# Reordering the first batch of an attention and MLP kernel: pooled k ahead of v, weight transposes during the divisions, and earlier scores in the later batches

## Chip, cores and metric

The kernel runs on one core of one Trainium2 chip. The metric is device time in microseconds (us), median over several executions; lower is better. Marks and durations come from one profiled execution of each kernel, which is about 1.8 us shorter than its time (374.2 against 375.95 us for the kernel before).

## The reference

For each of 8 batches, attention with keys and values mean-pooled over 8 neighbouring rows, then a residual MLP block that mixes first tokens, then channels:

```python
# q, k, v: (8, 8, 576, 64)
k_p = k.reshape(B, H, 72, 8, D).mean(axis=3)
v_p = v.reshape(B, H, 72, 8, D).mean(axis=3)
scores = np.matmul(q, k_p.transpose(0, 1, 3, 2)) / np.sqrt(D)
attn = softmax(scores)                       # (8, 8, 576, 72)
x = np.matmul(attn, v_p).transpose(0, 2, 1, 3).reshape(8, 576, 512)

tok = np.einsum('ts,bsd->btd', w_tok, alpha1 * x + beta1)
u   = x + lam * tok
ch  = np.maximum((alpha2 * u + beta2) @ w_ch1, 0) @ w_ch2   # 512 -> 2048 -> 512
out = u + lam * ch
```

## The kernel before

The order of instructions is written by hand. Batch 0 is a straight list, the opening. Then nine blocks of 512 tokens pass through the MLP (`mlp_A` is the first layer, `mlp_B` the second), and the attention of the next batch is woven between a block's matmuls at fractional slot numbers: slots 0 to 15 are the first layer, 16 to 31 the second.

| line | engine | work |
|---|---|---|
| L115, L117, L118 | GpSimd | `cast_rem`: the last 64 rows ("remainder") of q cast, of k summed |
| L132, L133 | VectorE or GpSimd | `sum_k`: rows of k summed in groups of 8 |
| L391, L395 | TensorE, copies | `att_K`: pooled k of four heads into its layout |
| L403, L405; L411, L415 | sums; TensorE, copies | `sum_v`, `att_V`: the same for v |
| L421, L422; L429, L431 | GpSimd; TensorE, copies | `sum_v_rem`, `att_Vrem`: remainder of v |
| L440, L442 | TensorE, ScalarE | `att_S`: scores and exponentials of a head |
| L457/L460, L462, L464 | TensorE, VectorE | `att_AV`: product with v, reciprocal, division into `x_tm` |
| L471, L475 | VectorE or GpSimd | `att_X`: `xs`, two heads of x times a row vector |
| L261 | VectorE | `row_of_xs`: one row of xs, from vectors alone |
| L276, L279 | TensorE, ScalarE | `setup_wtok`: token-mix weights transposed |
| L505, L520 | TensorE | `mix_T`, `mix_uT`: the token mix, and its result transposed |
| L536, L541; L559 | TensorE, ScalarE; TensorE | first layer and its relu; second layer |

The parts that the change touches:

```python
    def load_rem(b):
        raw = work.tile([P, 2, 4, D], FP, tag="rem_raw", bufs=2, name="rem_raw")
        for i, src in enumerate((q, k)):
            nc.sync.dma_start(out=raw[:, i]..., in_=src[b, :, 512:576, :]...)   # 128 KB each
# ...
    load_qk(0, 0)          # q and k of heads 0-3, 512 KB each
    load_rem(0)
    load_qk(0, 1)
    load_v(0, 0)
    load_v_rem(0)
    load_v(0, 1)
# ... the opening, from the first scores on
    sum_k(0, 1, nc.vector)
    att_F(0, 1)                            # q of heads 4-7 transposed
    att_S(0, 2)
    att_S(0, 3)
    sum_v(0, 0)
    att_Vrem(0, nc.scalar.copy)
    att_K(0, 1, nc.scalar.copy)
    att_V(0, 0, nc.vector.tensor_copy)
    sum_v(0, 1, nc.gpsimd)
    att_S(0, 4)
    att_AV(0, 0)
# ... heads 4 to 7 and the other products
    att_X(0, 4, 6, nc.gpsimd)
    load_w2(0)                             # 512 KB, a quarter of w_ch2
    setup_wtok(0, nc.scalar.copy)
    att_AV(0, 6)
    load_qk(1, 0, nc.vector)               # and the other loads of batch 1
# ...
    setup_rowsum(0)
    setup_wtok(2, nc.scalar.copy)
    setup_rowsum(1)
    setup_wtok(3, nc.scalar.copy)
    mix_T(0, 0)
    setup_rowsum(2)
    mix_T(0, 1)
    setup_rowsum(3)
    setup_vectors()
    mix_T(0, 2, nc.gpsimd)
# ... the later batches
    def attention(b):
        late = b == 1
        todo = [(2.0 if late else -2.0, lambda: cast_rem(b, nc.gpsimd)),
# ...
        for h in range(8):
            at = 13.6 + 1.0 * h if late else 13.1 + 1.0 * h
            todo.append((at, lambda h=h: att_S(b, h)))
            todo.append((at + 2.0, lambda h=h: att_AV(b, h)))
            if h % 2:
                todo.append((at + 2.1, lambda h=h: att_X(b, h - 1, h + 1)))
```

The softmax here doesn't subtract the row's maximum and nothing guards it: scores larger than these inputs give would overflow.

## Time and profile before

| | kernel before |
|---|---|
| time, median of 3 | 375.79 us (375.37 to 376.31) |
| span of the profiled execution | 374.2 us |
| busy: TensorE, VectorE, ScalarE, GpSimd | 355.8, 226.9, 203.8, 98.8 us |

I read this profile by marks: moments at which a stage starts on TensorE, found in its timeline. There are seven: first reciprocal (first L462), mix (first L505), A (first matmul of the first layer), B (first of the second layer), F2 and F7 (first transposes, L357, of q of batches 2 and 7), and the end. The sum of busy time is of less use. It comes from matmul records, and the trace of before lacks 43 of 2344.

### The profile page before, as it was taken

Reading aid. Unit: us, or ns where it says so; the run is one execution under the profiler, and the core shown is the slowest. Engines: PE = TensorE matmul, PEld = TensorE weight load, DVE = VectorE, ACT = ScalarE, POOL = GpSimd, SP = SyncE. Lnnn points to the kernel's source line nnn. Section 1 sums busy time; section 2 is a strip of 40 time slices with the busy share of each in tenths; the row PEclk is TensorE's granted clock in tenths of the full one; section 3 lists DMA queues with packets and bytes.
Section 4 is the critical chain, followed back from the end, with each engine's and each line's share of the span. In section 5 each row is a group of like instructions: output and inputs, shape, how many; then the busy total and the mean of one; then the engine's idle time right before and its main releaser. Section 6 shows DMA issues by size and latency. Waiting matters only on the chain.

```text
span 374.2 us, 6081 instructions
## 1 busy us (share of the span) xinstructions
PE 355.8 (95%) x2301; PEld 197.2 (53%) x2344; DVE 226.9 (61%) x468; ACT 203.8 (54%) x408; POOL 98.8 (26%) x145
## 2 busy tenths in 40 slices
PE   6589899999999999999999999999999999999995
PEld 2357555455545554555545554555455545544544
DVE  6585349783797269744985299428853797633011
ACT  4765885069704981399227941796159704712710
POOL 7774939004600470019000910073000000000000
PEclk9989999999999999999999999999999999999999
DMA  7999991039011912084016502480100011002002
GB/s 240 249 213 318 309 309 53 2 118 341 33 58 59 335 45 58 28 275 133 30 56 227 182 29 58 132 276 30 56 28 3 1 58 56 2 28 84 2 30 83
DMA packets 19602, 43.27 MB, mean 116 GB/s; under 512 B 2221, under 2 KB 4593, under 8 KB 19574
## 3 DMA queue, kind: packets, MB, share of 16 engines
q1 hardware_dynamic: 17488, 37.89, 29.9%
q0 software_dynamic: 1920, 4.86, 6.9%
q8 instruction: 18, 0.29, 0.3%
q10 hardware_dynamic: 166, 0.14, 0.1%
q14 instruction: 10, 0.08, 0.1%
HBM read 38.30 MB, written 9.44 MB: 128 GB/s over the span
## 4 chain that ended last, share of the span: by engine, by line
PE 77%; DVE 12%; DMA 5%; SPq 2%; ACT 1%; issue 1%; POOL 1%; POOLq 0%
PE ps_h L536 32%; PE ps_ch L559 25%; PE ps_tok L505 11%; DVE x_tm L464 5%; DVE xs L471 3%; PE ps_sc L440 3%; DMA rem_raw<-in_k_dram 2%; DMA rem_v_raw<-in_v_dram 2%; PE ps_uT L520 2%; PE ps_q L357 2%; DVE rec L462 1%; DVE xs L475 1%; PE ps_av L457 1%; SPq L78 1%; PE ps_kp L388 1%
## 5 line engine op out<-in xcount | busy, mean ns | idle before, releaser
L536 PE MATMUL ps_h<-u_fm,w 128*128 128x512 bf16 (+1 forms) x574 | 133.2, 373 | 1.0 <-ACT u_fm L522 0.2
L559 PE MATMUL ps_ch<-w,Hj 128*128 128x512 bf16 x493 | 123.2, 379 | 0.9
L541 ACT ACTIVATE Hj<-ps_h,bias_cols 128x512 bf16<-128x512 f32 x144 | 96.7, 691 | 38.2 <-PE ps_h L536 23.2
L536 PEld LDWEIGHTS <-w 128*128 128x128 bf16 x592 | 64.9, 114 | 48.0 <-issue 0.4
L559 PEld LDWEIGHTS <-Hj 128*128 128x128 bf16 x592 | 55.6, 98 | 48.6 <-issue 0.5
L522 ACT COPY u_fm<-ps_uT 128x512 bf16<-128x512 bf16 x36 | 21.1, 586 | 91.1 <-PE ps_uT L520 91.1
L442 ACT ACTIVATE ET<-ps_sc 128x288 f16<-128x288 f32 (+1 forms) x128 | 52.7, 488 | 12.5 <-PE ps_sc L440 11.8
L505 PE MATMUL ps_tok<-xs,wtT 128*128 128x512 bf16 (+1 forms) x196 | 48.5, 379 | 2.6 <-DVE xs L471 2.3
L395 DVE CAST kpT<-ps_kp 64x288 bf16<-64x288 f32 x29 | 13.2, 455 | 54.3 <-PE ps_kp L391 54.1
L115 POOL CAST rem_q<-rem_raw 128x256 bf16<-128x256 f32 x8 | 3.2, 398 | 140.3 <-DMA rem_raw<-in_q_dram 84.9
L566 DVE TENSOR_TENSOR u_sb<-u_sb,ps_ch 128x512 f32<-128x512 f32 (+1 forms) x37 | 24.9, 672 | 24.9 <-PE ps_ch L559 23.8
L565 DVE TENSOR_TENSOR ps_ch<-lam_bc,ps_ch 128x512 f32<-128x512 f32 x32 | 22.1, 691 | 19.8 <-PE ps_ch L559 19.5
L507 DVE TENSOR_TENSOR u_sb<-x_tm,ps_tok 128x512 f32<-128x512 f32 (+1 forms) x40 | 27.3, 684 | 10.4 <-PE ps_tok L505 10.3
L464 DVE TENSOR_TENSOR x_tm<-ps_av,rec 128x320 f32<-128x320 f32 x64 | 31.4, 491 | 2.3
L505 PEld LDWEIGHTS <-wtT 128*128 128x128 bf16 (+1 forms) x200 | 19.1, 98 | 25.2 <-issue 2.8
L440 PE MATMUL ps_sc<-qT,kpT 128*128 128x288 bf16 (+1 forms) x128 | 28.5, 306 | 2.1 <-ACT kpT L395 1.0
L132 POOL TENSOR_TENSOR qk_raw<-qk_raw 128x512 f32<-128x512 f32 (+1 forms) x28 | 28.8, 1029 | 3.4 <-DMA rem_raw<-in_k_dram 2.3
L509 DVE TENSOR_TENSOR u_bf<-u_sb,al_bc 128x512 bf16<-128x512 f32 (+1 forms) x39 | 27.9, 715 | 1.4
L462 DVE RECIPROCAL rec<-ps_av 128x5 f32<-128x5 f32 x64 | 12.0, 188 | 23.3 <-PE ps_av L460 22.9
L457 PEld LDWEIGHTS <-ET 72*128 72x128 f16 (+1 forms) x256 | 16.5, 100 | 15.5 <-DVE x_tm L464 1.0
L471 DVE TENSOR_TENSOR xs<-x_tm,lamal_bc 128x512 bf16<-128x512 f32 x29 | 21.6, 745 | 1.0
L457 PE MATMUL ps_av<-vp,ET 72*128 72x66 f16 (+1 forms) x256 | 18.7, 197 | 0.8 <-DVE x_tm L464 0.5
(111 smaller groups left out, 308.0 us busy)
## 6 DMA issues: line engine op xcount, KB each, us to landing
qk_raw<-in_q_dram SPq DMA_DIRECT2D x16, 512.0 KB, 5.7
qk_raw<-in_k_dram SPq DMA_DIRECT2D x16, 512.0 KB, 6.3
v_u<-in_v_dram SPq DMA_DIRECT2D x32, 256.0 KB, 7.2
out_dram<-u_sb SPq DMA_DIRECT2D x32, 256.0 KB, 2.3
w<-in_moe_w_ch_dram POOLq DMA_DIRECT2D x2, 1024.0 KB, 11.6
w<-in_moe_w_ch_dram POOLq DMA_DIRECT2D x4, 512.0 KB, 9.7
rem_raw<-in_q_dram SPq DMA_DIRECT2D x8, 128.0 KB, 8.3
rem_raw<-in_k_dram SPq DMA_DIRECT2D x8, 128.0 KB, 5.7
```

What stands on the lines that cost most here:

```text
L132: eng.tensor_tensor(out=t[:, :, 0:n], in0=t[:, :, 0:n], in1=t[:, :, n:2 * n], op=ALU.add)
L440: nc.tensor.matmul(out=ps_sc[0:n, 0:288], lhsT=kpT_pool[u][:, j, r, 72 * hh:72 * hh + n], rhs=st["qT"][u][:, h % 4, :])
L442: nc.scalar.activation(out=ET[0:n, 64 + j:64 + S + j:2], in_=ps_sc[0:n, 0:288], func=AF.Exp, bias=0.0, scale=1.0 / 64)
L457: nc.tensor.matmul(out=av[:, c, :], lhsT=ET[:, m0:m0 + 256:2], rhs=vp1)
L464: nc.vector.tensor_tensor(out=x[:, :, dd:dd + D], in0=av[:, :, 0:64], in1=rec.unsqueeze(2).to_broadcast((P, 5, D)), op=ALU.mult)
L471: eng.tensor_tensor(out=xs[:, 0:4, cols], in0=x[:, 0:4, cols], in1=lamal_bc[:, cols].unsqueeze(1).to_broadcast((P, 4, D * (h1 - h0))), op= ...
L505: nc.tensor.matmul(out=ps_tok, lhsT=wtT[0:kk, at, t0:t0 + P], rhs=xs[0:kk, sc, :], start=(sc == 0), stop=(sc == 4))
L507: nc.vector.tensor_tensor(out=s["u"][p0:p1, :], in0=st1[b]["x"][p0:p1, c, :], in1=ps_tok[p0:p1, 0:DM], op=ALU.add)
L509: eng.tensor_tensor(out=s["u_bf"][p0:p1, :], in0=s["u"][p0:p1, :], in1=al2_bc[p0:p1, :], op=ALU.mult)
L536: nc.tensor.matmul(out=ps_h[:, t0:t1], lhsT=w1_of(cc, j), rhs=u_fm[n][:, cc, t0:t1], start=(cc == 0), stop=(cc == 3))
L541: nc.scalar.activation(out=t, in_=ps_h, func=AF.Relu, bias=bias_cols[:, j:j + 1], scale=1.0)
L559: nc.tensor.matmul(out=ps, lhsT=Hj[n, j][:, 128 * m:128 * m + 128], rhs=w2_of(n, j, cols), start=(j == 0), stop=(j == NJ - 1))
```

## The change

Its intent: close TensorE's waits in the opening. Pooled k of heads 4 to 7 goes ahead of v; the remainders are loaded in another order and on another queue; the token-mix weights are transposed while VectorE divides; a quarter of the second layer's weights is loaded later, out of the way of batch 1's data; and scores of later batches start earlier, so that xs is ready for the mix.

```diff
-    def load_rem(b):
+    def load_rem(b, queue=nc.sync):
@@
+    load_rem(0, nc.scalar)
     nc.scalar.activation(out=start[:, 1:2], ... func=AF.Exp ...)
     load_qk(0, 0)
-    load_rem(0)
     load_qk(0, 1)
+    load_v_rem(0)
     load_v(0, 0)
-    load_v_rem(0)
     load_v(0, 1)
@@
-    row_of_xs(0, nc.vector)
     load_wtok()
@@
     att_F(0, 1)
+    att_K(0, 1, nc.vector.tensor_copy)
+    row_of_xs(0, nc.vector)
     att_S(0, 2)
+    att_Vrem(0, nc.vector.tensor_copy)
     att_S(0, 3)
     sum_v(0, 0)
-    att_Vrem(0, nc.scalar.copy)
-    att_K(0, 1, nc.scalar.copy)
     att_V(0, 0, nc.vector.tensor_copy)
@@  (heads 4 to 7: every score one step earlier; cut)
     att_S(0, 7)
+    att_V(0, 1, nc.scalar.copy)
+    setup_wtok(0, nc.scalar.copy)
     att_AV(0, 4)
+    setup_wtok(1, nc.scalar.copy)
     att_AV(0, 5)
-    load_w2(0)
@@  (loads of batch 1 two heads earlier, its remainder of v ahead of v; cut)
+    setup_wtok(2, nc.scalar.copy)
     att_AV(0, 6)
+    setup_rowsum(0)
+    setup_rowsum(1)
+    setup_wtok(3, nc.scalar.copy)
     att_AV(0, 7)
     att_X(0, 6, 8)
@@  (the other row sums, vectors and warm-up matmuls now lie ahead of the mix; cut)
-        todo = [(2.0 if late else -2.0, lambda: cast_rem(b, nc.gpsimd)),
+        todo = [(0.55 if late else -2.0, lambda: cast_rem(b, nc.gpsimd)),
@@
-            at = 13.6 + 1.0 * h if late else 13.1 + 1.0 * h
+            at = 13.0 + 1.0 * h if late else 11.7 + 1.05 * h
@@
-            for g in range(1, 4):
+            for g in range(4):
                 todo.append((3.0 + 1.5 * g, lambda g=g: load_w2(g)))
```

More of the change, by code (lines that the diff above doesn't have):

```diff
@@ L81, in load_qk @@
         st1[b]["raw"][u] = raw
-    def load_rem(b):
+    def load_rem(b, queue=nc.sync):
         raw = work.tile([P, 2, 4, D], FP, tag="rem_raw", bufs=2, name="rem_raw")
         for i, src in enumerate((q, k)):
-            nc.sync.dma_start(
+            queue.dma_start(
                 out=raw[:, i].rearrange("p c d -> p (c d)"),
@@ L608 @@
     att_AV(0, 0)
+    att_S(0, 5)
     att_AV(0, 1)
-    att_S(0, 5)
     att_AV(0, 2)
     att_X(0, 0, 2, nc.gpsimd)
+    att_S(0, 6)
     att_AV(0, 3)
     att_X(0, 2, 4, nc.gpsimd)
-    att_S(0, 6)
-    att_V(0, 1, nc.vector.tensor_copy)
     att_S(0, 7)
+    att_V(0, 1, nc.scalar.copy)
+    setup_wtok(0, nc.scalar.copy)
     att_AV(0, 4)
+    setup_wtok(1, nc.scalar.copy)
     att_AV(0, 5)
-    att_X(0, 4, 6, nc.gpsimd)
-    load_w2(0)
-    setup_wtok(0, nc.scalar.copy)
-    att_AV(0, 6)
     load_qk(1, 0, nc.vector)
@@ L626 @@
     load_qk(1, 1)
+    load_v_rem(1)
     load_v(1, 0)
-    load_v_rem(1)
     load_v(1, 1)
-    setup_wtok(1, nc.scalar.copy)
+    att_X(0, 4, 6, nc.gpsimd)
+    setup_wtok(2, nc.scalar.copy)
+    att_AV(0, 6)
+    setup_rowsum(0)
+    setup_rowsum(1)
+    setup_wtok(3, nc.scalar.copy)
     att_AV(0, 7)
     att_X(0, 6, 8)
-    setup_rowsum(0)
-    setup_wtok(2, nc.scalar.copy)
-    setup_rowsum(1)
-    setup_wtok(3, nc.scalar.copy)
-    mix_T(0, 0)
     setup_rowsum(2)
-    mix_T(0, 1)
     setup_rowsum(3)
     setup_vectors()
+    keep_warm(2)
+    mix_T(0, 0)
+    mix_T(0, 1)
     mix_T(0, 2, nc.gpsimd)
@@ L646 @@
     setup_bias(0)
-    keep_warm(2)
     for j in range(4):
```

## The prediction

> **What bounds the kernel now.** I read the page first, then the waits of TensorE, then the opening in order of time on each engine, then stretches of the later batches. In the page, the busy table and the slices come first:
>
> ```profile
> PE 355.8 (95%) x2301; PEld 197.2 (53%) x2344; DVE 226.9 (61%) x468; ACT 203.8 (54%) x408; POOL 98.8 (26%) x145
> PE   6589899999999999999999999999999999999995
> DMA  7999991039011912084016502480100011002002
> ```
>
> TensorE is busy 355.8 of 374.2 us, so all its idle time is 18.4 us. A slice is 9.4 us: only the first four or five and the last one have room. The table of stretches gives the room as stretch minus busy: 4.0 us in 0 to 12, 3.4 in 12 to 21.5, 1.3 in 21.5 to 32, 1.7 in 32 to 55.4, 0.8 in 55.4 to 79, and 4.2 in 345 to the end. A steady stretch such as the next one has only this:
>
> ```profile
> 78.95:118.20 39.25, 38.89 (x252) 21.44 (x256) 27.09 (x55) 22.37 (x46) 10.58 (x14) 1.00 0.39 131
> ```
>
> That is 0.36 us idle of 39.25, of which some 0.2 is one matmul record that the trace lacks. From 79 us on the kernel is bound by the amount of matmul work, which this change leaves as it is. The whole prize is therefore in the first 79 us, plus small change later. The waits of TensorE name it (columns: who, for whom; us in total, times, longest):
>
> ```profile
> PE ps_bc L255 <- DMA vecs<-in_moe_lam_dram: 2.7, 1, 2.7
> PE ps_tok L505 <- DVE xs L471: 2.3, 5, 0.9
> PE ps_v L429 <- POOL vrem L422: 2.0, 1, 2.0
> PE ps_sc L440 <- ACT kpT L395: 1.0, 1, 1.0
> PE ps_qr L372 <- POOL rem_q L115: 0.8, 1, 0.8
> ```
>
> The first is the launch and stays. The third and fourth are one story in the opening, which the timeline of the first batch shows (start, duration, engine, line, operation, and in brackets the idle time before):
>
> ```profile
> 14.26 1.30 POOL L421 TENSOR_TENSOR rem_v_raw<-rem_v_raw 64x256 f32<-64x256 f32 x2 [2.22 <-DMA rem_v_raw<-in_v_dram]
> 16.00 0.28 PE L429 MATMUL ps_v<-vrem,sel_rem 128*128 128x66 f16 x4 [2.04 <-POOL vrem L422]
> 16.12 0.38 PE L388 MATMUL ps_kp<-identity_bf,k_bf 128*128 128x128 bf16 x2
> 17.10 0.81 ACT L395 CAST kpT<-ps_kp 64x288 bf16<-64x288 f32 x2
> 17.54 0.87 PE L440 MATMUL ps_sc<-qT,kpT 128*72 128x288 bf16 x2 [0.96 <-ACT kpT L395]
> 18.72 0.20 DVE L462 RECIPROCAL rec<-ps_av 128x5 f32<-128x5 f32 x1 [1.49 <-PE ps_av L460]
> ```
>
> The remainder of v lands at 14.26, behind both halves of v's first load. TensorE stands before its pooling for 2.04 us; the pooled k of heads 4 to 7 stands behind it in program order, though its sums were ready at 13.3; ScalarE copies v's remainder, then k; scores of head 4 start at 17.54. The divisions begin at 18.72 and are then a VectorE chain, eight pairs at a pitch of 0.63 us.
>
> **What the Trainium skill says.** "Perfetto Trace Analysis", section "Identifying the Most-Contended Engine", warns that matmul busy time is no measure of distance to the roofline; I use it only for the idle gaps, and look at the path before each gap. "DMA: Bandwidth & Descriptors", section "Issuing engines are not separate DMA queues": transfers started by sync, scalar or gpsimd run on the same 16 engines and interleave, so another queue saves issue time only. The trace agrees that the engines are what is full: DMA share 1.02 in 10 to 20 us, 1.12 in 20 to 30. "GPSIMD Engine Reference", section "1. Specifications", says its memory interfaces are shared with VectorE, with contention where VectorE has two inputs in memory. The trace agrees: the multiply that makes xs takes 1.26 us on VectorE at 60.41 while GpSimd pools k, and 0.69 at 63.82 beside its smaller sums. "TensorE: Matmul & The Clock Gate", Part 1, says the array starts at half rate until sustained activity. It agrees: four products with v take 0.43 us at 18.20 and 0.29 at 21.57, and the granted clock is 0.82 in 12 to 21.5.
>
> **The change part by part.**
>
> *Loads of batch 0.* The remainders of q and k move to ScalarE's queue (two issues of 0.6 us, ahead of its table load of 1.28; its first copy is at 4.81, so it slips 0.1 or 0.2). By the page above this shares bandwidth with k's first load, which lands at 7.73 and starts the chain. 256 KB at about 290 GB/s (estimate from 1.9 MB between 7.73 and 14.26) are 0.9 us if all of it got ahead; I take half, 0.4 later. The remainder of v now goes before v: ahead of 512 KB, so about 12.1 instead of 14.26, and v about 0.8 later.
>
> *Pooling on VectorE.* Pooled k no longer waits for v. But VectorE gets two copies of k (0.81) and two of v's remainder (0.75 on ScalarE) ahead of the sums of v. My ledger for VectorE: sums of k 8.2 to 10.0, first copies to 11.4, sums of the second half (1.15 + 0.43) to 13.0, a wait for TensorE of 0.7, the copies to 14.6, the row of xs 0.68 to 15.3, v's remainder to 16.0, sums of v (1.15 + 0.70) to 17.8, TensorE 0.35, copies 0.6, and the first product with v at about 18.8, its reciprocal at 19.2. Scores of head 4 stand behind v's pooling, at about 18. So **the divisions start no sooner, perhaps 0.5 later**: the idle 1.43 and 1.49 us of VectorE are filled with 1.56 of copies and a later load.
>
> *Divisions.* One pair of copies (0.60 at 21.24) leaves VectorE for ScalarE: its chain is 5.05 instead of 5.7. But ScalarE now has, from head 4's exponentials on, 3.4 of exponentials, 0.5 of v, four transposed-weight copies of 0.65 and the row sums of 0.26 before the mix: 7.1 us to the last weight copy, about 25.3 if it never waits. GpSimd's three xs pairs take 1.65 each after head 1, and end near 25.5. Three engines end close together, so **the mix starts between 25.3 and 26.0, against 25.50**.
>
> *Mix to the first layer.* Before, from 25.50 to the first matmul of the first layer at 32.05 are 6.55 us. Four mixes at 1.08 are 4.32, two transposes 0.45, the bias 0.70: 5.47. The other 1.08 are the two row sums, the vectors and the warm-up matmuls between them, which now lie before the mix. First layer at about 31.2: **0.85 saved**, half of it hoped for.
>
> *Batch 1.* Its loads are started two heads earlier and the 512 KB of the second layer's weights no longer compete. The sum of k waits until 35.06 now; 0.52 MB at 311 GB/s (32 to 55 us) are 1.7 us, so about 33.4. The cast of the remainder of q now comes before these sums, so TensorE's wait at 38.35 goes: **0.83 saved**.
>
> *Batch 1's scores* 0.6 slot sooner: that stretch has waits of 0.29 (scores behind ScalarE), 0.53 and 0.20 (VectorE's divisions and xs): **0.5 saved**.
>
> *Batches 2 to 7.* Scores start at 11.7 instead of 13.1, the last xs a slot sooner before the mix at 25. That can take away the four later waits of ps_tok, 2.3 - 0.9 - 0.2 = 1.2 us. Against it: more exponentials fall into the first layer, where ScalarE is busy 3.63 of 3.70 us (91.70 to 95.40). Pitch there by the trace: a relu 0.57 and two exponentials 0.67 are 1.24 per slot on ScalarE, against 0.86 + 0.25 + 0.15 = 1.26 on TensorE. It just fits; I charge 0.5 for all six. **0.7 saved.**
>
> Sum: 0.85 + 0.83 + 0.5 + 0.7 = 2.9, so 375.8 - 2.9 = 372.9; I say 372.7, as a sooner warm clock would help a little.
>
> **Rivals.** First, the opening gains fully: if k's first load is not delayed and v comes in good time, the divisions start 1 us or more before 18.72, and all after it moves; that makes 370 to 371. For it: TensorE's 2.04 + 0.96. Against it: VectorE's ledger. Second, ScalarE becomes the bound of the first layer in batches 2 to 7: six times 0.3 to 0.6 us of waits on PSUM buffers cancels the opening: 374 to 376. For it: 3.63 of 3.70 busy. Against it: 1.24 against 1.26. Third, the weights of the second layer come too late: they are now issued in slots 3 to 7.5, and the second layer starts near 54. An issue at about 38 plus 9.7 us to landing is 48, so no. Fourth, a large gain over 2% (7.5 us) would need nearly all idle time between 10 and 310 us; no single wait offers it.
>
> **Range and chances.** The four terms each have about their own size as error; together some 2 us either way. Range 370.0 to 375.2. Faster by over 2% needs 368.4: 0.04. Slower by over 2% needs 383: 0.02. Within: 0.94.
>
> **What will show it.** Right: TensorE's wait for the pooled remainder of v shrinks to under 0.5; first reciprocal near 19; mix near 25.6; first layer near 31.2 (32.05 before); wait for rem_q gone; stretches of later batches 39.1 long or a little less, without waits of ps_tok. Wrong: the first reciprocal at 17.5 or sooner (my ledger for VectorE too pessimistic), waits of ps_h or ps_sc for ScalarE in every batch, or k's first sum after 8.6.

## The result, and the profile after

The changed kernel took 379.87 us (median of 4: 379.0, 379.01, 380.73, 381.28), the kernel before on the same chip 375.95. Its time over that of before is 1.0109, with a 95% interval of 1.0069 to 1.0150. (Ratios here are the mean time of one kernel's runs over that of the other's in the same rounds, so not quite the ratio of the medians.) That is a loss of about 1%, where a gain of 0.8% was predicted, and outside the predicted range.

The page of the changed kernel, its busy table and slices:

```profile
PE 360.0 (95%) x2344; PEld 197.6 (52%) x2344; DVE 232.9 (62%) x470; ACT 200.1 (53%) x406; POOL 100.9 (27%) x145
...
PE   6579999999999999999999999999999999999995
...
DMA  7999695029210922076015601390110011002002
```

No matmul record is missing here, so 360.0 against 355.8 is no growth of work. VectorE, with two more instructions, is busy 6.0 us longer. About 1.2 of that is copies exchanged with ScalarE (0.92 + 0.86 taken over, 0.60 given away); most of the rest is instructions that have become longer. In the DMA row a 6 stands in the fifth slice (38 to 47 us) where there was a 9, and a 5 in the seventh where there was a 1: loads leave a hole and end later.

The waits of TensorE after the change (for whom, for what; total us, times, longest):

```profile
PE ps_v L411 <- DVE v_sum L405: 3.8, 1, 3.8
...
PE ps_kp L391 <- POOL rem_k L118: 1.2, 1, 1.2
PE ps_sc L440 <- ACT Hj L541: 0.9, 1, 0.9
PE ps_tok L505 <- DVE xs L471: 0.8, 1, 0.8
```

The wait for the pooled remainder of v (2.0 before) is gone, as was the aim. A wait of 3.8 for VectorE's sums of v stands in its place, with 1.2 for the remainder of k, which was not among before's. Of the waits for xs only one is left, in batch 1.

Marks of both traces, in us from the start of the span:

| | first reciprocal | mix | A | B | F2 | F7 | end |
|---|---|---|---|---|---|---|---|
| before | 18.72 | 25.50 | 32.05 | 55.35 | 81.54 | 277.76 | 374.2 |
| after | 21.35 | 28.68 | 34.30 | 56.54 | 83.52 | 280.92 | 377.2 |
| after is later by | 2.63 | 3.18 | 2.25 | 1.19 | 1.98 | 3.16 | 3.0 |

The third row shows a loss of 3.18 up to the mix. Of it 0.93 is regained from the mix to A and 1.06 from A to B; gains in those two places were predicted. From B to F2 0.79 is lost and from F2 to F7 1.18.

The opening of the changed kernel in its timeline (start, duration, engine, line, operation, and in brackets the idle time before and what ended it; ACTq is the queue on which ScalarE starts transfers):

```profile
2.88 0.61 ACTq L87 DMA_DIRECT2D rem_raw<-in_k_dram  x1
...
6.92 1.08 DVE L132 TENSOR_TENSOR qk_raw<-qk_raw 128x512 f32<-128x512 f32 x2
...
10.23 0.45 POOL L117 TENSOR_TENSOR rem_raw<-rem_raw 128x128 f32<-128x128 f32 x1 [1.44 <-DMA rem_raw<-in_k_dram]
...
11.27 0.21 PE L391 MATMUL ps_kp<-pool_rem,rem_k 128*128 128x32 bf16 x1 [1.18 <-POOL rem_k L118]
...
12.09 1.54 DVE L132 TENSOR_TENSOR qk_raw<-qk_raw 128x512 f32<-128x512 f32 x2
...
13.66 0.83 DVE L133 TENSOR_TENSOR k_bf<-qk_raw 128x256 bf16<-128x256 f32 x1
...
15.22 0.92 DVE L395 CAST kpT<-ps_kp 64x288 bf16<-64x288 f32 x2 [0.73 <-PE ps_kp L391]
...
16.16 0.98 DVE L261 TENSOR_TENSOR xs<-vecs 1x512 bf16<-1x512 f32 x1
16.72 2.67 POOL L403 TENSOR_TENSOR v_u<-v_u 128x512 f32<-128x512 f32 x2
17.07 0.86 DVE L431 CAST vp<-ps_v 8x264 f16<-8x264 f32 x2
17.96 1.71 DVE L403 TENSOR_TENSOR v_u<-v_u 128x512 f32<-128x512 f32 x2
...
20.19 0.29 PE L411 MATMUL ps_v<-v_sum,sel_main 128*128 128x128 f16 x1 [3.79 <-DVE v_sum L405]
...
21.35 0.20 DVE L462 RECIPROCAL rec<-ps_av 128x5 f32<-128x5 f32 x1 [0.22 <-PE ps_av L460]
```

Two things are to be seen. The remainder of k, started at 2.88 (2.97 before), could be summed only from 10.23 (8.78 before), while k's first load was there at 6.92 (7.73 before; other kernels with the old queue have 6.81 to 7.83 too, so that difference is scatter). And from 12.09 on VectorE hardly stops: pooled k, the row of xs, v's remainder and v itself stand in one file, each longer than in the trace before. At 20.19 TensorE has waited 3.79 us. For comparison, the row and the second half of k in before:

```profile
10.96 0.68 DVE L261 TENSOR_TENSOR xs<-vecs 1x512 bf16<-1x512 f32 x1
11.68 1.15 DVE L132 TENSOR_TENSOR qk_raw<-qk_raw 128x512 f32<-128x512 f32 x2
```

And further on in the changed kernel, ScalarE's copy of v (heads 4 to 7) and the division that follows it on VectorE:

```profile
24.07 0.53 ACT L415 CAST vp<-ps_v 64x128 f16<-64x128 f32 x2
24.71 0.20 DVE L462 RECIPROCAL rec<-ps_av 128x5 f32<-128x5 f32 x1 [0.63 <-PE ps_av L460]
```

### The profile page after: what moved, and what is told of

Its sections match the earlier page's. It is cut to its first block, busy times and chain, and to the rows that moved or that the text cites. A ratio compares the mean times of both kernels' runs of the same rounds, so it can differ in the third digit from the quotient of the medians.

```text
span 377.2 us, 6105 instructions
## 1 busy us (share of the span) xinstructions
PE 360.0 (95%) x2344; PEld 197.6 (52%) x2344; DVE 232.9 (62%) x470; ACT 200.1 (53%) x406; POOL 100.9 (27%) x145
## 4 chain that ended last, share of the span: by engine, by line
PE 79%; ACT 12%; DVE 5%; DMA 2%; issue 1%; ACTq 1%; POOL 0%
PE ps_ch L559 31%; PE ps_h L536 26%; PE ps_tok L505 11%; ACT Hj L541 5%; PE ps_sc L440 3%; PE ps_uT L520 2%; DMA rem_raw<-in_k_dram 2%; PE ps_av L457 2%; ACT ET L442 2%; ACT qT L361 1%; ACT vp L431 1%; DVE xs L471 1%; PE ps_q L357 1%; DVE x_tm L464 1%; ACT wtT L279 1%
## 5 line engine op out<-in xcount | busy, mean ns | idle before, releaser
L536 PE MATMUL ps_h<-u_fm,w 128*128 128x512 bf16 (+1 forms) x592 | 135.6, 373 | 0.8 <-ACT u_fm L522 0.4
L559 PE MATMUL ps_ch<-w,Hj 128*128 128x512 bf16 x512 | 125.0, 379 | 0.0
L559 PEld LDWEIGHTS <-Hj 128*128 128x128 bf16 x592 | 54.8, 98 | 50.6 <-issue 1.1
L395 DVE CAST kpT<-ps_kp 64x288 bf16<-64x288 f32 x31 | 14.1, 455 | 58.1 <-PE ps_kp L391 57.9
L440 PE MATMUL ps_sc<-qT,kpT 128*128 128x288 bf16 (+1 forms) x128 | 29.4, 306 | 1.4 <-ACT Hj L541 0.9
L471 DVE TENSOR_TENSOR xs<-x_tm,lamal_bc 128x512 bf16<-128x512 f32 x29 | 23.4, 807 | 0.8
```

Of the source, the lines that this page charges most:

```text
L440: nc.tensor.matmul(out=ps_sc[0:n, 0:288], lhsT=kpT_pool[u][:, j, r, 72 * hh:72 * hh + n], rhs=st["qT"][u][:, h % 4, :])
L471: eng.tensor_tensor(out=xs[:, 0:4, cols], in0=x[:, 0:4, cols], in1=lamal_bc[:, cols].unsqueeze(1).to_broadcast((P, 4, D * (h1 - h0))), op= ...
L536: nc.tensor.matmul(out=ps_h[:, t0:t1], lhsT=w1_of(cc, j), rhs=u_fm[n][:, cc, t0:t1], start=(cc == 0), stop=(cc == 3))
L559: nc.tensor.matmul(out=ps, lhsT=Hj[n, j][:, 128 * m:128 * m + 128], rhs=w2_of(n, j, cols), start=(j == 0), stop=(j == NJ - 1))
```

## The experiments

Theory after the first look: (1) the remainder's new queue, (2) VectorE's file ahead of v, (3) the moved weight load, (4) the earlier scores each cost something, and the re-placed transposes themselves gain. The rival: the transposes during the divisions, the core of the change, are what costs. Five rounds each, always with the kernel before on the same chip. "In after" means that one part of the changed kernel is undone; "in before" that one part of the change is done alone.

### a_rem_sync: the remainder back on its queue, in after

```diff
-    load_rem(0, nc.scalar)
     load_qk(0, 0)
+    load_rem(0)
     load_qk(0, 1)
```

> The changed kernel with one edit: the remainders of q and k of batch 0 are again issued by the sync engine, between the two halves, not by ScalarE. Theory A (the other queue delays the remainder of k, and with it the first pooled k): the sums of k's remainder start before 9.0 us instead of 10.23, TensorE's wait of 1.18 us for them goes, the first reciprocal comes 0.8 to 1.3 us before 21.35, and the time falls by 0.6 to 1.3 us. Rival (VectorE's chain alone sets the divisions): the remainder lands sooner, but the first reciprocal moves by less than 0.3 us and the time by less than 0.4.

Measured: 379.37 us, ratio to before 1.0078 (1.0052 to 1.0104). The timeline of this run:

```profile
7.82 0.62 POOL L117 TENSOR_TENSOR rem_raw<-rem_raw 128x128 f32<-128x128 f32 x1
...
14.35 2.39 DVE L261 TENSOR_TENSOR xs<-vecs 1x512 bf16<-1x512 f32 x1
```

The sums of the remainder of k start at 7.82 instead of 10.23, the wait of 1.18 is gone, first scores are at 10.38 instead of 12.02. But the first reciprocal comes only 0.95 sooner (20.40): the row of xs, 0.68 in the trace before, here takes 2.39 beside GpSimd's work and stands ahead of v. So by this pair of profiles the queue costs about a microsecond in the opening, and VectorE's file takes back the rest. From B to F2 this run needs 28.21 us (after: 26.98), with waits of up to 1.6 for `x_tm`; that comes up again below.

### a_dve_light: VectorE relieved, in after

```diff
     keep_warm(2)
+    row_of_xs(0, nc.vector)            # while VectorE waits for TensorE
     att_Frem(0, (0,), nc.scalar.copy)
@@
     att_K(0, 1, nc.vector.tensor_copy)
-    row_of_xs(0, nc.vector)
     att_S(0, 2)
-    att_Vrem(0, nc.vector.tensor_copy)
+    att_Vrem(0, nc.scalar.copy)
```

> The changed kernel with VectorE relieved in the opening: the remainder of v is copied by ScalarE as in the kernel before, and the row of xs is made in VectorE's idle time before the first copy of k. Theory (work put ahead of the sums of v on VectorE is what delays the divisions): 0.98 + 0.86 us leave its path, TensorE's wait of 3.79 us before v's pooling shrinks to about 2, the first reciprocal comes 1.5 to 1.9 us before 21.35, and the time falls by 1.2 to 2.0 us. Rival (v lands late, so the sums of v cannot start sooner): the sums still start near 17.9 after an idle gap of VectorE, and the time stays within 0.4.

Measured: 379.97 us, 1.0093 (1.0065 to 1.0120). TensorE's wait for the sums of v falls from 3.79 to 2.66, the first reciprocal comes 0.49 sooner. That is less than the 1.84 us (0.98 + 0.86) taken out of the file. The remainder of k landed 0.26 later in this run, and the sums of k that follow took 2.10 where after has 1.54; the sums of v began 1.14 sooner (16.82 against 17.96), but took 2.80 instead of 2.14. So v had landed, and the rival is out; but in the time no effect is shown, since the interval includes after's 1.0109.

### a_late_scores and b_soon_scores: the earlier scores of batches 2 to 7

```diff
-            at = 13.0 + 1.0 * h if late else 11.7 + 1.05 * h
+            at = 13.0 + 1.0 * h if late else 13.1 + 1.0 * h      # a_late_scores, in after
-            at = 13.6 + 1.0 * h if late else 13.1 + 1.0 * h
+            at = 13.6 + 1.0 * h if late else 11.7 + 1.05 * h     # b_soon_scores, in before
```

> The changed kernel with the scores of batches 2 to 7 at their old slots (13.1 + 1.0 h). Theory (the sooner scores fill ScalarE in the first layer and cost TensorE small waits): the distance between the first transposes of batches 2 and 7 goes from 197.4 back to 196.2 us as before, so the time falls by 0.9 to 1.4 us. Rival (that stretch is lost for another reason, for instance the other order of loads): it stays at 197.4 and the time within 0.4.

> The kernel before with only the scores of batches 2 to 7 sooner (11.7 + 1.05 h). Theory: the waits of the mix for xs vanish (1.2 us) but waits behind ScalarE cost more: the time rises by 0.9 to 1.4 us. As I had predicted: it falls by about 0.7. Rival (no effect): within 0.4.

Measured: a_late_scores 380.3 us, 1.0109 (1.0084 to 1.0133), no better than after; b_soon_scores 377.05, 1.0018 (0.9992 to 1.0043). From F2 to F7 (five batches) before needs 196.22 us and b_soon_scores 197.39, as much as after (197.40). So in before the earlier scores cost 1.17 us over this stretch, although every wait for xs is gone. (The whole time, 1.0018, does not show it clear of noise.) The stretches from q's second transpose in the block to B of that block, first in before, then in b_soon_scores (stretch, length; busy us and instructions of TensorE, weight loads, VectorE, ScalarE, GpSimd; granted clock, DMA share, GB/s):

```profile
88.57:95.39 6.82, 6.77 (x48) 4.24 (x47) 0.96 (x3) 6.75 (x15) 6.00 (x9) 1.00 0.89 305
```

```profile
88.61:96.77 8.16, 8.04 (x62) 4.97 (x61) 2.93 (x7) 8.12 (x20) 6.94 (x9) 1.00 0.76 261
```

With two more heads of scores (0.25 each by their pitch) and two more products with v (0.15 each), the stretch should be 6.82 + 0.80 = 7.62 long; it is 8.16. ScalarE is busy 8.12 of these 8.16 us: it sets the pace, 0.54 us are lost, and every single wait of TensorE is too short for the trace to list. The waits for xs that went were worth 0.9 from F2 to F7 (0.48 + 0.41; a third, of 0.28, lies after F7). 1.17 + 0.9 over five batches is 0.41 a batch, near the 0.54 seen here.

a_late_scores missed its expectation: its F2 to F7 is 197.21, not 196.2, and its time did not fall, which is what its rival said. Two things stand in its trace: the waits for xs come back, 2.7 us of them in place of 0.8, and batch 1 runs into the collision of the next experiments (B to F2 28.76). The old slots give 196.18 to 196.37 from F2 to F7 in six other kernels (before among them), but 197.47 in a_undone_xs1. So the cost of the earlier scores is shown in before; that after would get it back by undoing them alone is not.

### a_w2_old: the weight load back in its old place, in after

```diff
     att_X(0, 4, 6, nc.gpsimd)
+    load_w2(0)
@@
-            for g in range(4):
+            for g in range(1, 4):
```

> The changed kernel with one edit: the first quarter of the second layer's weights is again issued right after the third xs pair (about 27 us), not in slot 3 of the first block (40.2 us). Theory (with that load moved, the DMA engines have nothing queued at 38 to 42 us, where the changed kernel moves 68 GB/s; batch 2's loads then land 4 us later, and GpSimd pools them on top of the xs multiplies of batch 1): the DMA share in 38 to 42 us is above 0.9 instead of 0.33, GpSimd's cast of batch 2's remainder starts by 53 us instead of 55.3, the stretch from the first matmul of the second layer to the first transposes of batch 2 goes from 27.0 (up to 28.8 in other runs) to 26.2 us, and the mean time falls by 0.8 to 2.0 us. Against it batch 1's k lands 1.7 us later. Rival (xs is slow for another reason): share in the gap rises, but the stretch stays at 27 or more and the time within 0.4.

Measured: 379.0 us, 1.0063 (1.0040 to 1.0087); 0.46 of the 1.09 per cent are gone. The row for 38 to 42 us of the stretches in before, after and a_w2_old:

```profile
38.00:42.00 4.00, 3.60 (x20) 2.12 (x22) 1.31 (x3) 2.80 (x5) 3.83 (x7) 1.00 1.07 333
```

```profile
38.00:42.00 4.00, 4.00 (x47) 3.07 (x45) 0.12 (x1) 4.00 (x9) 3.84 (x7) 1.00 0.33 68
```

```profile
38.00:42.00 4.00, 3.76 (x47) 3.29 (x46) 0.00 (x0) 3.25 (x7) 3.76 (x6) 1.00 0.89 308
```

Here the loads of batch 1 are done in after, and the weights have not been started: the DMA engines move 68 GB/s where before they moved 333. That is 265 GB/s times 4 us, about 1.06 MB, which has to be moved later. Three weight loads, 1.5 MB, then start together at 40.2, in the same moment as batch 2's loads. With one load back in its old place the hole is gone (308 GB/s). (a_w2_old reached A 1.42 us later; the same stretch counted from A is 36.58 to 40.58 in after, and moves 179 GB/s there.) What the hole does downstream shows on GpSimd (sums of k of batch 2, heads 4 to 7), VectorE (third multiply for xs of batch 1) and TensorE (mix of batch 1); first before, then after:

```profile
59.86 2.40 POOL L132 TENSOR_TENSOR qk_raw<-qk_raw 128x512 f32<-128x512 f32 x2
...
63.82 0.69 DVE L471 TENSOR_TENSOR xs<-x_tm,lamal_bc 128x512 bf16<-128x512 f32 x1
...
67.13 1.24 PE L505 MATMUL ps_tok<-xs,wtT 128*128 128x512 bf16 x5 [0.20 <-DVE xs L471]
```

```profile
64.39 2.40 POOL L132 TENSOR_TENSOR qk_raw<-qk_raw 128x512 f32<-128x512 f32 x2
...
64.94 1.26 DVE L471 TENSOR_TENSOR xs<-x_tm,lamal_bc 128x512 bf16<-128x512 f32 x1
...
69.10 1.24 PE L505 MATMUL ps_tok<-xs,wtT 128*128 128x512 bf16 x5 [0.82 <-DVE xs L471]
```

In before GpSimd's sums of k are over when VectorE's third multiply starts, and it is at the smaller ones for v's remainder. In after the sums of k lie over it, it takes 1.26 instead of 0.69, and the mix waits 0.82 instead of 0.20. I measure this shift as the start of GpSimd's first sums of k of batch 2, counted from B: 0.28 us in before, 3.58 in after, 0.97 in a_w2_old. B to F2 goes with it in these three: 26.19, 26.98, 26.40 us. It does not simply grow with the shift: at 2.7 to 2.9 (a_rem_sync, b_weights_k, a_late_scores) it is 28.2 to 28.8, since there the sums lie over the first two pairs of multiplies. A caution: the opening of a_w2_old, the same program as after's, was 1.03 us later at the first reciprocal. That much does one execution scatter, so I rest on stretches within a run and on ratios over six runs, not on single marks.

### a_four_undone: all four parts undone, in after

The edit is the four diffs above that begin with a_. The transposes during the divisions, pooled k ahead of v and the new order of batch 1's loads stay.

> The changed kernel with four causes undone at once: remainders of q and k on the sync queue, VectorE relieved of v's remainder and the row of xs, second-layer weights at the old place, scores of batches 2 to 7 at the old slots. What is left of the change: the pooled k of heads 4 to 7 ahead of v, v's remainder loaded ahead of v, transposed weights during the divisions, batch 1's loads and scores a little sooner. Theory (these four are all of the loss): within 0.8 us of the kernel before, or faster by up to 1.5. Rival (something else in it costs too): still 1.5 us or more slower.

Measured: 377.25 us, 1.0009 (0.9982 to 1.0037). Taken one by one the four are worth 0.31 + 0.16 + 0.46 + 0.00 = 0.93 per cent, together 1.00. Each of these has an interval of about a quarter of a per cent either way, so the shares are rough, and that the two sums agree is in part luck. Clear of noise is the whole: the loss of the change is in these four parts, and the rival, the transposes, is not what costs. But the gain that A and B promise (A at 32.03, level with before; B at 54.27, 1.08 sooner) doesn't reach the end either: F2 is 0.63 sooner, the span 0.5.

### b_weights_early and b_weights_k: the good parts alone, in before

```diff
 # b_weights_early: before, with the lines of after from att_S(0, 4) to mix_uT((0, 1)); and
     mix_T(0, 3)
+    load_w2(0)
@@
-        todo = [(2.0 if late else -2.0, lambda: cast_rem(b, nc.gpsimd)),
+        todo = [(0.55 if late else -2.0, lambda: cast_rem(b, nc.gpsimd)),
 # b_weights_k: that, and
     att_F(0, 1)
+    att_K(0, 1, nc.scalar.copy)
     att_S(0, 2)
```

> The kernel before with the part of the change that I had counted on: transposed weights and row sums before the mix, batch 1's loads two heads earlier, its cast of the remainder ahead of its sums; the first quarter of the second layer's weights issued after the fourth mix (about 32 us), so that the DMA engines neither stand idle at 38 to 42 us nor carry it ahead of batch 1's k. All else as before. Theory (by my own step 'mix to the first layer' and 'batch 1'): mix to first layer 5.6 us instead of 6.55, the wait of 0.83 us for batch 1's remainder gone, the second layer starts near 54 instead of 55.4, and the time falls by 1.0 to 1.8 us. Rival (the DMA engines set batch 1 and what is gained before is waited for there): the second layer starts at 55.2 or later and the time stays within 0.5.

> As the one above, and the pooled k of heads 4 to 7 right after its queries, copied by ScalarE, so that its scores do not stand behind the remainder of v. Theory: scores of head 4 no longer wait for the copies of k (0.96 us), the first reciprocal comes 0.5 to 1 us sooner than 18.7, and the time is 0.3 to 1.0 us below that of the run above. Rival (the divisions are set by the sums of v, slowed by GpSimd at the same time): the first reciprocal stays near 18.7 and the time within 0.3 of the run above.

Measured: 375.84 us, 0.9978 (0.9954 to 1.0003), and 376.24 us, 0.9994 (0.9968 to 1.0020). In time neither gain is clear of noise, and both expectations were missed. The transposes gain what was hoped: mix to A is 5.62 and 5.61 us (6.55 before), B at 54.85 and 54.15 (55.35 before). In b_weights_early TensorE waits 0.88 in batch 1 for GpSimd's pooled k, so its A to B stays at 23.34. Pooled k ahead of v brought nothing here (one trace each): the first reciprocal is at 18.86 with it and 18.20 without, as the rival said of that mark, and TensorE then waits 2.2 us for the sums of v. Then it is lost again: B to F2 takes 27.06 and 28.27 us, where before takes 26.19. In b_weights_k all four VectorE instructions for the first two xs pairs of batch 1 have 1.26 to 1.57 us, and TensorE waits 1.56 once for `x_tm`. GpSimd's sums of k start 1.63 and 2.74 us after B in these two (0.28 in before): B has moved ahead, GpSimd's pooling of batch 2 has not. An earlier B brings nothing, if that pooling then lies over VectorE's xs.

### a_xs_pool and b_xs_pool: one xs pair to GpSimd, ahead of batch 2's pooling

If the third xs pair of batch 1 is on GpSimd, it stands in GpSimd's program ahead of the pooling of batch 2. The trace of a_xs_pool shows that order kept: GpSimd idles 14.96 us until the pair starts at 63.83, and only then pools. So the pooling can't lie over the earlier pairs.

```diff
-                todo.append((at + 2.1, lambda h=h: att_X(b, h - 1, h + 1)))
+                todo.append((at + 2.1, lambda h=h: att_X(b, h - 1, h + 1,
+                    nc.gpsimd if late and h == 5 else nc.vector)))      # a_xs_pool, in after
+                    nc.gpsimd if h == 5 else nc.vector)))               # b_xs_pool, in before: every batch
```

> The changed kernel with one edit: in batch 1 the third pair of xs multiplies (heads 4 and 5) is made by GpSimd. It stands in GpSimd's order ahead of the pooling of batch 2, so that pooling starts only after it, near 66 us, and no longer runs on top of VectorE's first two xs pairs; the pooled data are needed at 83 us only. Theory (this overlap is the second loss, and what makes the changed kernel's times scatter): VectorE's xs multiplies of 256 columns take 0.7 us each instead of 0.75 to 1.57, the waits of TensorE for the divisions (0.47) and for xs (0.82) go, the stretch from the second layer's first matmul to batch 2's first transposes falls from 27.0 to 25.6 or 26.0, and the mean falls by 1.0 to 2.0 us. Rival (the overlap is harmless): stretch 26.8 or more, time within 0.4.

> The kernel before, with the third xs pair of every batch from 1 on made by GpSimd. Theory: its waits for xs in the first block and in batches 3, 5 and 7 (0.2, 0.5, 0.4, 0.3) and the wait of 0.53 for the divisions go, the time falls by 0.8 to 1.8 us, 0.2 to 0.5 per cent. Rival (GpSimd, 1.7 us for the pair, ends later than VectorE would have): the mix waits for GpSimd instead and the time stays within 0.4.

Measured: a_xs_pool 378.57 us (378.05 to 378.92), 1.0056 (1.0039 to 1.0072); b_xs_pool 378.8, 1.0065 (1.0047 to 1.0083). The timeline of a_late_scores, where the collision is at its worst, and that of a_xs_pool:

```profile
62.70 1.57 DVE L471 TENSOR_TENSOR xs<-x_tm,lamal_bc 128x512 bf16<-128x512 f32 x1
...
66.36 0.30 PE L457 MATMUL ps_av<-vp,ET 72*128 72x66 f16 x4 [1.56 <-DVE x_tm L464]
```

```profile
61.26 0.69 DVE L471 TENSOR_TENSOR xs<-x_tm,lamal_bc 128x512 bf16<-128x512 f32 x1
...
65.69 0.40 POOL L115 CAST rem_q<-rem_raw 128x256 bf16<-128x256 f32 x1
```

The same multiply takes 1.57 us beside GpSimd's sums and 0.69 without them. In a_xs_pool the pooling starts only at 65.69, the waits for xs and `x_tm` there are gone, and B to F2 falls from 26.98 to 26.15. (A new wait of 0.76 us, for the mixed rows `u_bf`, stands just ahead of F2.) The scatter of the times shrinks from 2.3 us to 0.9. That after's two groups of times, near 379 and near 381, are light and bad cases of the collision is a guess: one profile of each kernel can't show it, and before's eleven times in one set of rounds spread over 3.1 us.

In all batches the same move is bad: F2 to F7 takes 199.43 us in b_xs_pool, 3.2 more than before. Its trace lists 11 waits of transposes for `u_bf`, 3.8 us in sum (3.0 of it from F2 to F7), where before's lists none.

### c_early_xs and c_k_xs: the same in all batches, with the good parts

b_weights_early and b_weights_k with the edit of b_xs_pool.

> The version b_weights_early with the third xs pair of batches 1 to 7 on GpSimd. Theory: the second layer starts near 54.2 as there or a little later, the stretch after it falls from 27.1 to about 25.8, the waits of later batches go; the time is 2 to 3 us below the kernel before (0.5 to 0.8 per cent). Rival: within 0.8 us of it.

> The version b_weights_k with the third xs pair of batches 1 to 7 on GpSimd. Theory: as c_early_xs, and some tenths below it if the earlier scores of heads 4 to 7 count at all; 2 to 3.5 us below the kernel before. Rival: equal to or above c_early_xs, since the divisions are set by the sums of v.

Measured: 377.39 us, 1.0022 (1.0004 to 1.0040), and 376.7 us, 1.0010 (0.9991 to 1.0028). F2 is reached at 80.53 and 80.36, a microsecond ahead of before, as hoped; and F2 to F7 takes 199.4 in both, as in b_xs_pool. A miss as versions, but it said what to run next.

### c_early_xs1, c_k_xs1 and a_undone_xs1: the xs pair moved in batch 1 alone

b_weights_early, b_weights_k and a_four_undone with the edit of a_xs_pool (`late and h == 5`).

> The kernel before with the token-mix weights transposed during the divisions, and the third xs pair of batch 1 alone on GpSimd. If the overlap of batch 2's pooling (GpSimd) with batch 1's xs (VectorE) is a cost by itself, the stretch from the first second-layer matmul to batch 2's mark shrinks from the 27.06 us of the same kernel without the move to about 26.2, and, other than with the move in all batches (199.4), the stretch from batch 2 to batch 7 stays at 196.2: span about 373.4, ratio to the kernel before 0.995 to 0.998. If the earlier gain of that stretch came only with the move in all batches, it stays near 27.

> The same with the pooled k of heads 4 to 7 ahead of v as well. That kernel without the move had 28.27 us from the second layer to batch 2. If the overlap is the cost: 26.2, batch 2 to 7 at 196.2, span about 373.2, ratio 0.994 to 0.998. If something else makes that stretch long, 27 or more and a ratio of 0.998 to 1.001.

> The changed kernel with the four suspects undone, and the third xs pair of batch 1 on GpSimd. The four undone had 26.64 us from the second layer to batch 2, and 196.37 from there to batch 7. If the overlap is the last of the costs: 26.2, 196.3, span about 373.2, ratio 0.995 to 0.999, which would leave nothing of the 1.1 per cent. If the ratio stays at 1.001 or more, a cost of the change is not yet found.

| kernel | time, us | ratio to before (95%) | B to F2 | F2 to F7 |
|---|---|---|---|---|
| before, same rounds | 376.48 | | 26.19 | 196.22 |
| c_early_xs1 | 375.24 | 0.9968 (0.9943 to 0.9994) | 26.14 | 196.26 |
| c_k_xs1 | 374.57 | 0.9954 (0.9928 to 0.9980) | 26.14 | 196.37 |
| a_undone_xs1 | 376.56 | 1.0012 (0.9980 to 1.0043) | 26.15 | 197.47 |

(The stretches of before are from its first profile.) Without the move B to F2 was 27.06, 28.27 and 26.64, so the collision is a cost of that stretch by itself, in kernels with the opening of before as well. In the whole time its cost is less sharp: with and without the move 0.9968 and 0.9978, 0.9954 and 0.9994, 1.0012 and 1.0009, all with overlapping intervals. The timeline of c_k_xs1 at first reciprocal, A and B:

```profile
17.77 0.20 DVE L462 RECIPROCAL rec<-ps_av 128x5 f32<-128x5 f32 x1 [0.23 <-PE ps_av L460]
...
31.05 1.03 PE L536 MATMUL ps_h<-u_fm,w 128*128 128x256 bf16 x8 [0.17 <-ACT u_fm L522]
...
53.34 1.02 PE L559 MATMUL ps_ch<-w,Hj 128*128 128x512 bf16 x4
```

A is 1.00 us and B 2.01 us ahead of before, F2 2.06, and the end, 372.2, still 2.0. Some of that is luck: the same opening had its first reciprocal at 18.86 and 18.93 in b_weights_k and c_k_xs. The ratio of 0.9954 rests on six executions. Both c_ kernels with the move in batch 1 are faster than the kernel before in the same rounds, by a third to a half of a per cent; the changed kernel, in other rounds, was 1.1% slower than it.

a_undone_xs1 missed its expectation (0.995 to 0.999). Its B to F2 is as expected; its F2 to F7 is 1.1 us longer than that of c_k_xs1 with the same program for these batches. Two waits for xs, in batches 2 and 3, are 0.60 and 0.72 long (0.28 and 0.33 in c_k_xs1), which is 0.71 of it. VectorE's first multiply for xs takes 1.20 and 1.08 us in these two batches, 0.69 in c_k_xs1. So the collision goes on in later batches, by how the engines happen to stand to each other; what sets that stays open.

## Why the prediction was wrong

**Right, and close in size.** Mix to A: 0.93 saved, 0.85 predicted; it is 5.61 or 5.62 us in all 14 kernels with the transposes moved, 6.55 to 7.27 in the three without. The wait for the remainder of q in batch 1 went, and A to B is 1.06 shorter, 0.83 predicted. In after that can be luck: b_soon_scores, with before's program there, lacks the wait too and has 22.30, its A being 1.05 later than before's. a_four_undone, with A at 32.03, shows that the change gives it without a late A. The waits for xs in later batches went, worth 1.2 (three waits, not the four that the prediction counts). The wait for the pooled remainder of v went.

**The first failed step: "this shares bandwidth with k's first load, which lands at 7.73 and starts the chain ... I take half, 0.4 later".** The wrong transfer was taken for the victim. k's first load was not delayed: its sums start at 6.90 to 7.46 us in the five kernels with the new queue, at 6.81 to 7.83 in the twelve with the old. The remainder itself came 1.45 later than before (10.23 against 8.78), though issued 0.1 sooner. a_rem_sync shows it: 2.4 us sooner with the old queue. Over all kernels its sums start at 7.68 to 8.93 with the old queue, at 10.10 to 11.26 with the new. "DMA: Bandwidth & Descriptors", section "Queues, rings and completion order", says that an engine goes round between the queues packet by packet. On SyncE's queue the remainder was issued ahead of k's and q's second loads; on another queue it shares the engines with them all. The landing agrees with that; which packets went in between, no run shows.

**The second, and the largest: VectorE's ledger, "its reciprocal at 19.2".** It was 21.35. By the timeline, the second half of k began at 12.09 instead of 11.4, its sums took 2.37 instead of 1.58, the row 0.98 instead of 0.68, v's remainder 0.86 instead of 0.7, the sums of v 2.14 instead of 1.85. That is 0.7 + 0.8 + 0.3 + 0.15 + 0.3, together 2.2. The list of instructions and the order were right. The durations came from moments at which GpSimd had no sums to make (all but the 0.70), and in the changed order it sums the remainder of v from 13.26 to 15.19 and v from 16.72 to 19.99 beside them. That this overlap made them longer is read from the trace; no run takes GpSimd's sums away in the opening, as a_xs_pool does in batch 1. And the trace of before was one of several cases: in b_soon_scores, with the same opening, v's remainder was there at 12.44, VectorE's sums of v took 4.0 us instead of 1.85, and the first reciprocal came at 18.66 all the same. The prediction had cited the shared memory interfaces of "GPSIMD Engine Reference", "1. Specifications", for xs, and had not used them in its own sum.

**The third: the divisions.** The mix was to follow the first reciprocal by 6.1 to 6.8 us; it took 7.33, and 7.33 to 7.69 in the kernels that have the transposes and before's opening (6.78 to 7.18 in the three kernels without the transposes). "Its chain is 5.05 instead of 5.7" was the step: from the first reciprocal to the end of the last division VectorE took 6.24 us (5.83 before). It stands idle for 0.63 at 24.71, since the copy of v that was moved to ScalarE runs there from 24.07 to 24.60 and TensorE's product waits for it; all kernels with that copy on ScalarE show this gap, of 0.63 to 0.76. The mix starts about 0.2 us after the last multiply for xs. TensorE's wait of 0.6 for ScalarE's copies of the weights is over at 27.72, that multiply only at 28.50, so this wait costs little. So this part brings 0.93 after the mix and costs some 0.15 to 0.9 ahead of it.

**The fourth: the third rival, "An issue at about 38 plus 9.7 us to landing is 48, so no".** The weights were in time, as it says. But the question asked was only whether they are late. What mattered was when they use the DMA engines: they leave a hole at 38 to 42 us and then run beside batch 2's data; GpSimd's pooling, 3.3 us later against B, moves over VectorE's xs, and B to F2 lost 0.79. The step "Batch 1's scores ... 0.5 saved" failed with it: of its three waits the one behind ScalarE (0.29) grew to 0.90, the one for the divisions went from 0.53 to 0.47, the one for xs from 0.20 to 0.82. The wait behind ScalarE is 0.90 or 0.91 in every kernel that starts batch 1's scores sooner, 0.28 or 0.29 in all others; no run undoes that part alone.

**The fifth: "It just fits; I charge 0.5 for all six".** In b_soon_scores the charge was 0.41 to 0.54 for each batch. The pitch of 1.24 against 1.26 counted only scores and relus. ScalarE was already busy 6.75 of 6.82 us in that stretch; the second rival came nearest, within its own 0.3 to 0.6.

Against the working of the sum: 0.85 + 0.83 came (0.93 + 1.06), 0.5 became a loss of 0.79, 0.7 a loss of 1.18 from F2 to F7, and the opening, put at zero to half a microsecond, lost 3.18 by the mix.

## What to carry to other kernels

When an instruction moves, take its duration from a place where the same neighbours run: here two-input work of VectorE took up to twice as long and more beside GpSimd (a multiply 0.69 and up to 1.57 us), and that is most of what turned a ledger of 19.2 into 21.35. When a transfer moves, ask not only whether it lands in time but what it leaves idle and whom it pushes, and whose work then lies over whose. And a gain in one stage counts only when the next stage's mark has moved as well: here an earlier B was twice eaten up before F2, until one pair of multiplies was put ahead of the pooling to keep the two engines apart.

## What the Trainium skill lacked or had wrong

- "GPSIMD Engine Reference", "1. Specifications": names the contention with two-input VectorE work, but no size, and no other page has one for these instructions. Here the multiply for xs took 0.69 us without and 1.26 to 1.57 beside GpSimd's sums of k over 128 partitions, but 0.69 also beside its sums of v's remainder over 64; a 1x512 multiply took 0.68 and up to 2.39.
- "DMA: Bandwidth & Descriptors", "Issuing engines are not separate DMA queues": says that another issuing engine saves issue time only. Here it also changed the time of arrival: the remainder of k, issued 0.1 us sooner on ScalarE's queue, could be used 1.45 us later. That a small urgent transfer came sooner from the queue of the large ones, ahead of them, stands on no page.
- "Perfetto Trace Analysis", "Optimization Strategy": its advice on finding the gaps of the busiest engine misses waits that are too short to be listed. ScalarE's pace cost TensorE 0.54 us in a stretch of 8.16 in which no wait of TensorE is listed; only the length of the stretch shows it.
- No page has how far the opening of one program scatters from one execution to the next: the first reciprocal of the same opening came at 17.77, 18.86 and 18.93 us, and k's first load could be summed from 6.81 to 7.83 us in twelve kernels that issue it alike.
